# Attention over induced points into a ReLU² MLP: last batch's output chunk by chunk, the closing check moved into the next stage, products earlier, a fourth buffer of x

## The chip, the cores and the metric

The kernel runs on one core of a Trainium2 chip. The metric is device time in microseconds for one execution, as the median of several runs. The engines of the core are named as in the profile: PE (TensorE, matmuls; PEld is its loading of weights), DVE (VectorE), ACT (ScalarE), POOL (GpSimd) and SP (SyncE, which here issues the DMAs). "Clock" is the TensorE clock that the throttle granted, as a share of full speed.

## The reference

Four batches of 12480 rows with 128 features are reduced by attention with 32 inducing vectors, read back by attention, and passed through an MLP with a squared ReLU.

```python
x: (4, 12480, 128) f32    inducing: (32, 128) f32
w_in: (128, 2048)         w_out: (2048, 128)

def mab(q, kv):
    s = scale * (q @ kv.transpose(0, 2, 1))
    s = s - s.max(-1, keepdims=True)
    a = np.exp(s)
    a /= a.sum(-1, keepdims=True) + 1e-09
    return a @ kv
h = mab(I, x)             # (4, 32, 128): 32 rows attend over 12480
y = mab(x, h)             # (4, 12480, 128): each row attends over 32
g = np.maximum(y @ w_in, 0.0) ** 2
out = g @ w_out           # (49920, 128)
```

## The kernel before

Each batch is cut into 26 chunks of 480 rows (`CH`), and its loads into 7 groups `G` of four chunks, the last of two. Two layouts of x are read: `xT` (features on the partitions, tile `xp`) for the scores, and `xn` (rows on the partitions, tile `xn`) for the sum that gives h.

For a batch `b` there is a **first** part (L271): the scores of the 32 inducing vectors (PE at L266, DVE at L281), their maximum, the exponentials on ACT (L304), a transpose on DVE (L313), and `hacc` (PE at L321), which multiplies them with one `xn` tile per group and adds up h in `hq` (L328, L330). `xn` has `XB = 3` buffers: three groups are loaded ahead by `loads`, and group G + 3 is issued behind the matmuls of group G (L325).

Then **prepare** (L374). The MLP is not run column by column. The 32 attention weights of a row are close to equal, so y @ w_in differs little from its mean; hidden columns that can't change sign are treated in closed form. Their squares are a quadratic form in the attention weights, and the kernel builds its matrix `w16` once per batch in four blocks c = 0 to 3: DVE makes products `G` of the 32 columns of h @ w_in with shifted copies of themselves (L544, four instructions a block, and a cast at L546 for the last), and PE multiplies them with w_out (`wq`, L550); DVE or ACT scales the result into `w16`, and DVE takes its largest size `wm` (L552). `G` has two buffers. The few columns that can change sign ("hot") sit in the last 16 rows of block 3. At the end prepare closes a check of the precision (L557 to L574): some nine small DVE instructions on 128x1 values (`wx`, `cm2`), two transposes on PE (L570), and a flag per batch. All flags are read after the last batch; were one zero, a slow way through the whole MLP would be taken instead.

**second** (L351) turns a group's scores into centred f16 attention weights `d16` (ACT at L360 and L364, PE at L367, DVE at L368).

The main loop runs over 13 duos (pairs of chunks) a batch. For each duo there are four steps j in the order 3, 0, 1, 2: `up` multiplies `d16` with a constant matrix of differences into a PSUM tile `hp` of two banks (L593, two buffers); `lift` squares it into `g` (ACT at L602 for j = 0 to 2; for j = 3 DVE makes `tmp` at L606 and POOL squares it at L607). `down` of the duo before adds up the output tile `po`, two banks and one buffer: `lin` for both chunks (L614, 32 rows of the array for each), then for each of four blocks the matmul of both chunks (L618), then one eviction of both chunks, 960 columns, on DVE (L624) for duos below 7 and on ACT (L622) from 7 on, and one store of 480 KB.

Beside this loop `background(b, c)` gives out the work of batch b + 1: each piece is a generator, and `give` advances it to a number of steps that grows with c, the duo plus the quarter. Scores run up to c = 3.5, the rest of the first part up to 6, prepare from 6 on. Text order is only a rank: a planner in the framework turns it into the order on each engine by its own costs, and may put a later instruction first where it expects an engine to be free. Each engine then runs its instructions in order, with waits.

Batch 0 has no loop to hide beside: its first part and prepare run at the start, among the loads and the narrowing of the weights from 64 to 32 bits on DVE (`narrow`, L212 to L224), which uses the pool `start`. That pool is closed before the main loop, and the pool `mlp` takes its place.

## Time and profile before

| | |
|---|---|
| runs | 475.28, 481.98, 489.18 us; median 481.98 |
| profiled execution | 469.63 us, span 467.8 us |
| PE / DVE / ACT / POOL busy | 363.1 / 316.4 / 245.4 / 95.1 us |
| mean granted clock of PE | 0.91 |
| moved by DMA | 81.58 MB |
| start of the main loop's squares | about 100 us |
| last eviction | 457.79 to 458.94 us |

The profile is of one execution. A row of the timeline gives start and duration in us, engine, line, operation, output and inputs, shape and count, and in brackets the engine's idle time before it with what ended it. A row of the waits gives the waiting instruction, the releaser, and the total, the count and the longest in us. Idle time of an engine that isn't on the chain costs nothing. Times of matmuls are pipelined: a matmul of 480 columns shows 0.37 us, but several behind each other follow every 0.2 us.

### The profile page before, as it was taken

Reading aid. Unit: us, or ns where it says so; the run is one execution under the profiler, and the core shown is the slowest. Engines: PE = TensorE matmul, PEld = TensorE weight load, DVE = VectorE, ACT = ScalarE, POOL = GpSimd, SP = SyncE. Lnnn points to the kernel's source line nnn. Section 1 sums busy time; section 2 is a strip of 40 time slices with the busy share of each in tenths; the row PEclk is TensorE's granted clock in tenths of the full one; section 3 lists DMA queues with packets and bytes.
Section 4 is the critical chain, followed back from the end, with each engine's and each line's share of the span. In section 5 each row is a group of like instructions: output and inputs, shape, how many; then the busy total and the mean of one; then the engine's idle time right before and its main releaser. Section 6 shows DMA issues by size and latency. Waiting matters only on the chain.

```text
span 467.8 us, 7805 instructions
## 1 busy us (share of the span) xinstructions
PE 363.1 (78%) x2967; PEld 158.3 (34%) x2967; DVE 316.4 (68%) x836; ACT 245.4 (52%) x338; POOL 95.1 (20%) x62
## 2 busy tenths in 40 slices
PE   3654284598987989889869979799889888888871
PEld 0133141462243424422433346222434264222220
DVE  4779936778675579966755696856755879666420
ACT  1040022634574567765834485565644757676780
POOL 1000000013313113222221121333221222244430
PEclk9986567589999998999998988899999979899997
DMA  8999758000169778122596882222751211232232
GB/s 315 415 401 339 238 197 350 1 1 30 62 234 333 294 277 292 45 84 85 195 312 212 338 285 94 85 85 83 242 183 43 86 42 43 85 127 106 111 125 98
DMA packets 18184, 81.58 MB, mean 174 GB/s; under 512 B 2000, under 2 KB 4048, under 8 KB 18128
## 3 DMA queue, kind: packets, MB, share of 16 engines
q1 hardware_dynamic: 18128, 80.90, 46.9%
q8 instruction: 27, 0.44, 0.4%
q14 instruction: 29, 0.24, 0.2%
HBM read 55.33 MB, written 25.56 MB: 173 GB/s over the span
## 4 chain that ended last, share of the span: by engine, by line
PE 54%; DVE 26%; DMA 9%; ACT 6%; issue 3%; SPq 1%; ACTq 0%; DVEq 0%
PE po L618 15%; PE s L266 12%; PE hp L593 8%; DMA xn<-xn_dram 6%; PE hacc L321 4%; DVE tmp L606 3%; PE hwv L385 3%; DVE G L544 3%; ACT g L602 3%; PE R L495 3%; DMA xp_False<-xT_dram 3%; PE po L614 2%; ACT o L622 2%; PE kv L501 1%; DVE o L624 1%
## 5 line engine op out<-in xcount | busy, mean ns | idle before, releaser
L602 ACT ACTIVATE g<-hp 128x960 f16<-128x960 f32 x156 | 143.1, 969 | 93.7 <-PE hp L593 93.5
L607 POOL TENSOR_TENSOR g<-tmp 128x960 f16<-128x960 f32 x52 | 93.8, 1803 | 357.6 <-DVE tmp L606 242.1
L618 PE MATMUL po<-g,w 128*128 128x480 f16 x416 | 113.0, 380 | 0.0
L606 DVE TENSOR_SCALAR tmp<-hp,off,cut 128x960 f32<-128x960 f32 x52 | 66.1, 1271 | 35.6 <-PE hp L593 35.6
L593 PE MATMUL hp<-d,pairs 32*128 32x480 f16 x312 | 60.9, 377 | 14.9 <-ACT g L602 10.0
L321 PE MATMUL hacc<-xn,en 128*32 128x128 f32 (+1 forms) x840 | 33.8, 303 | 22.4 <-DMA xn<-xn_dram 9.9
L618 PEld LDWEIGHTS <-w 128*128 128x128 f16 x416 | 33.8, 101 | 47.3 <-issue 30.4
L266 PE MATMUL s<-xp_False,indT_sb 128*32 128x480 f32 x208 | 38.5, 701 | 12.2 <-DMA xp_False<-xT_dram 9.8
L172 ACT ACTIVATE s<-s 128x480 f32<-128x480 f32 (+1 forms) x27 | 15.4, 569 | 46.0 <-PE s L266 46.0
L622 ACT ACTIVATE o<-po,bias,osc 128x960 f32<-128x960 f32 x24 | 27.6, 1152 | 20.8 <-PE po L618 20.7
L321 PEld LDWEIGHTS hacc<-xn,en 128*32 128x32 f32 (+1 forms) x840 | 27.0, 120 | 30.7 <-issue 19.9
L593 PEld LDWEIGHTS <-pairs 32*128 32x128 f16 x312 | 14.8, 92 | 66.5 <-issue 65.3
L624 DVE TENSOR_SCALAR o<-po,osc,bias 128x960 f32<-128x960 f32 x28 | 35.4, 1264 | 0.0
L281 DVE TENSOR_SCALAR_CACHE_REDUCE sT<-s 128x480 f32<-128x480 f32 (+1 forms) x28 | 18.3, 654 | 21.4 <-PE s L266 21.3
L304 ACT ACTIVATE sT<-sT,nb 128x480 f32<-128x480 f32 (+1 forms) x28 | 19.1, 682 | 25.3 <-DVE nb L298 25.3
L397 DVE TENSOR_REDUCE bm<-s 128x1 f32<-128x480 f32 (+1 forms) x28 | 18.2, 650 | 19.9 <-ACT s L172 19.6
L266 PE MATMUL s<-xp_False,dhT 128*32 128x480 f32 x208 | 29.2, 648 | 1.2 <-DVE dhT L348 1.2
L544 DVE TENSOR_TENSOR G<-hwp,hw 128x512 f16<-128x512 f16 x64 | 27.9, 458 | 0.7 <-PE wq L550 0.7
L614 PE MATMUL po<-d,lin 32*128 32x480 f16 x104 | 21.0, 367 | 7.8 <-ACT o L622 7.2
L550 PE MATMUL wq<-w_hi,G 128*128 128x128 f16 x256 | 18.4, 230 | 4.0 <-DVE G L546 3.4
L360 ACT ACTIVATE s<-s,nb 128x480 f32<-128x480 f32 (+1 forms) x28 | 17.8, 688 | 5.6 <-DVE k L438 5.6
L330 DVE TENSOR_TENSOR hq<-hacc,hq 128x128 f32<-128x128 f32 x24 | 6.8, 284 | 20.4 <-PE hacc L321 20.2
(227 smaller groups left out, 415.4 us busy)
## 6 DMA issues: line engine op xcount, KB each, us to landing
outT_dram<-o SPq DMA_DIRECT2D x52, 480.0 KB, 2.6
xp_False<-xT_dram SPq DMA_DIRECT2D x24, 960.0 KB, 7.5
xn<-xn_dram SPq DMA_DIRECT2D x24, 960.0 KB, 7.4
wi<-w_in_dram SPq DMA_DIRECT2D x4, 512.0 KB, 13.4
wo<-w_out_dram SPq DMA_DIRECT2D x4, 512.0 KB, 12.0
xp_False<-xT_dram SPq DMA_DIRECT2D x4, 480.0 KB, 6.1
xn<-xn_dram SPq DMA_DIRECT2D x4, 480.0 KB, 9.0
indT_sb<-indT_dram SPq DMA_DIRECT2D x1, 16.0 KB, 1.8
```

The costliest lines, as they stand in the source:

```text
L266: nc.tensor.matmul(ps[32 * q:32 * q + 32, 0:CH], lhsT, xp[:, q, :], start=True, stop=True)
L304: nc.scalar.activation(sT[G][0:r], sT[G][0:r], AF.Exp, bias=nb[0:r], accum_out=st.zs[0:r, G:G + 1])
L321: st.last = nc.tensor.matmul(hacc[c:c + 32, 0:P], en[0:r, k, :], xg[0:r, k, :], start=k < 4, stop=k >= NBLK - 4,)
L544: tt(g[:, :, MI * j:MI * j + n], hwp[:, :, 0:n], hw16f[:, :, s0:s0 + n], op=ALU.mult)
L593: nc.tensor.matmul(hp[:, i, 0:CH], w[r], st.d16[self.G][r], start=True, stop=True)
L602: nc.scalar.activation(self.g[:, j], hp[:, :, 0:CH], AF.Square)
L606: nc.vector.tensor_scalar(tmp, hp[:, :, 0:CH], st.off, cut, op0=ALU.add, op1=ALU.max)
L607: nc.gpsimd.tensor_tensor(self.g[:, j], tmp, tmp, op=ALU.mult)
L614: nc.tensor.matmul(po[:, i, 0:CH], st.lin[r], st.d16[self.G][r], start=True, stop=False)
L618: nc.tensor.matmul(po[:, i, 0:CH], st.w16[:, j], self.g[:, j, i], start=False, stop=n == NC - 1)
L622: nc.scalar.activation(o, po[:, :, 0:CH], AF.Identity, bias=st.bias, scale=st.osc)
L624: nc.vector.tensor_scalar(o, po[:, :, 0:CH], st.osc, st.bias, op0=ALU.mult, op1=ALU.add)
```

## The change

1. `XB` goes from 3 to 4: `loads` fetches four tiles of `xn` ahead, in batch 0 too, and group G + 4 is issued behind the matmuls of group G. For the room `wo_sb` (the narrowed w_out, needed at the start only) moves from the pool `const` to `start`.
2. The products `G` of block 0 are given right behind the scan that ends the preparation of the columns (L475), those of block 1 behind `cat` (L497), and those of block c + 2 behind the matmuls of block c. The buffers of `G` stay two. Prepare now has 25 steps, of which `N_PRE = 26` covers the last.
3. The closing of the check becomes a generator of its own, `closing(b)`, with two steps: the DVE chain is given when batch b's own loop reaches c = 1, the transposes and the flag at c = 2. It was the last part of prepare, ahead of batch b's first duo.
4. For batch 3 `down_singly` takes the place of `down`: lin and the four blocks of chunk 0, its eviction of 480 columns on DVE and its store of 240 KB, then the same for chunk 1, in six steps. The `po` tile and its one buffer stay.

```diff
-XB = 3
+XB = 4
...
-    wo_sb = const.tile([P, NF, P], F32, name="wo_sb")
...
     start = start_pools.enter_context(tc.tile_pool(name="start", bufs=1))
+    wo_sb = start.tile([P, NF, P], F32, name="wo_sb")
...
         nc.vector.tensor_tensor_scan(inc, onec, mix, 0.0, op0=ALU.mult, op1=ALU.add)
         yield
 
+        gs = {}
+
+        def products(c):
+            g = gs[c] = flow.tile([P, NF, P], F16, tag="G", name=f"G_{b}_{c}", bufs=2)
+            for j in range(4):
+                s0 = 4 * c + j + 1
+                n = MI if s0 < 16 else MX
+                tt(g[:, :, MI * j:MI * j + n], hwp[:, :, 0:n], hw16f[:, :, s0:s0 + n], op=ALU.mult)
+            if c == NC - 1:
+                nc.vector.tensor_copy(g[:, :, P - MX:P], hot[:, :, MX:2 * MX])
+
+        products(0)
+        yield
...
         nc.vector.tensor_copy(cat, ps[0:MI + 2, 0:P])
+        products(1)
         yield
...
-        wm = small("wm5", NC)
+        wm = st.wm = small("wm5", NC)
         for c in range(NC):
-            g = flow.tile([P, NF, P], F16, tag="G", name=f"G_{b}_{c}", bufs=2)
-            for j in range(4):
-                s0 = 4 * c + j + 1
-                n = MI if s0 < 16 else MX
-                tt(g[:, :, MI * j:MI * j + n], hwp[:, :, 0:n], hw16f[:, :, s0:s0 + n], op=ALU.mult)
-            if c == NC - 1:
-                nc.vector.tensor_copy(g[:, :, P - MX:P], hot[:, :, MX:2 * MX])
-            yield
             ps = att_psum(f"wq_{b}_{c}")
             for k in range(NF):
-                nc.tensor.matmul(ps[:, 0:P], g[:, k], w_hi[:, k], start=k == 0, stop=k == NF - 1)
+                nc.tensor.matmul(ps[:, 0:P], gs[c][:, k], w_hi[:, k], start=k == 0, stop=k == NF - 1)
             evac(st.w16[:, c], ps[:, 0:P], P, wsc if c < NC - 1 else wsn)
             nc.vector.tensor_reduce(wm[:, c:c + 1], ps[:, 0:P], axis=AX.X, op=ALU.max, apply_absolute_value=True)
             yield
-
+            if c + 2 < NC:
+                products(c + 2)
+                yield
+        st.kept = kv_, rho, pr, cm2
+
+    def closing(b):
+        st = sts[b]
+        tt, ts, stt = nc.vector.tensor_tensor, nc.vector.tensor_scalar, nc.vector.scalar_tensor_tensor
+        kv_, rho, pr, cm2 = st.kept
 
         wx = small("wx")
-        nc.vector.tensor_reduce(wx, wm, axis=AX.X, op=ALU.max)
+        nc.vector.tensor_reduce(wx, st.wm, axis=AX.X, op=ALU.max)
...
+        def down_singly(self):
+            st = self.st
+            po = ps_o.tile([P, 2, 512], F32, tag="po", name=f"po_{self.b}_{self.d}")
+            for i in range(2):
+                r = self.rows(i)
+                nc.tensor.matmul(po[:, i, 0:CH], st.lin[r], st.d16[self.G][r], start=True, stop=False)
+                for n, j in enumerate((3, 0, 1, 2)):
+                    nc.tensor.matmul(po[:, i, 0:CH], st.w16[:, j], self.g[:, j, i], start=False, stop=n == NC - 1)
+                    if n % 2 == 0:
+                        yield
+                o = mlp.tile([P, 2, CH], F32, tag="o", name=f"o_{self.b}_{self.d}_{i}", bufs=3)
+                nc.vector.tensor_scalar(o[:, i], po[:, i, 0:CH], st.osc, st.bias, op0=ALU.mult, op1=ALU.add)
+                nc.sync.dma_start(outT[:, self.b, 2 * self.d + i, :], o[:, i])
+                yield
+
         def down(self):
+            if self.b == NB - 1:
+                yield from self.down_singly()
+                return
...
-    N_LOADS, N_SCORES, N_HEADS, N_PRE, N_SECOND = NG + XB, NG, 2 + 1 + 2 * NG + 2, 7 + 18, 2
+    N_LOADS, N_SCORES, N_HEADS, N_PRE, N_SECOND = NG + XB, NG, 2 + 1 + 2 * NG + 2, 26, 2
...
+    for b in range(NB):
+        gens["c", b] = closing(b)
...
     def background(b, c):
 
+        give(("c", b), 0 if c < 1 else 1 if c < 2 else 2)
```

## The prediction

> **What bounds the kernel now.** I read the page first, then the table by stretches, then the waits, and last the timeline round the places that the change touches.

> ```profile
> span 467.8 us, 7805 instructions
> PE 363.1 (78%) x2967; PEld 158.3 (34%) x2967; DVE 316.4 (68%) x836; ACT 245.4 (52%) x338; POOL 95.1 (20%) x62
> PE 54%; DVE 26%; DMA 9%; ACT 6%; issue 3%; SPq 1%; ACTq 0%; DVEq 0%
> ```

> TensorE (PE) carries over half of the chain and is the busiest engine, at 78%. So the question is where PE stands still. In the next fence the columns are stretch, length, busy time and count of PE, PEld, DVE, ACT and POOL, then the granted clock, the DMA share and GB/s.

> ```profile
> 0.00:40.00 40.00, 19.45 (x175) 7.38 (x175) 28.94 (x104) 6.14 (x15) 1.28 (x10) 0.90 0.97 380
> 110.00:122.00 12.00, 11.70 (x73) 2.75 (x67) 8.88 (x18) 4.93 (x6) 3.39 (x2) 1.00 0.11 42
> 134.00:146.00 12.00, 8.90 (x153) 4.62 (x144) 6.43 (x13) 5.90 (x7) 2.31 (x2) 1.00 0.99 336
> ```

> The start is held by DMA (share 0.97). After it, batch 0's first duos fill PE (11.70 of 12 us), but in the stage that accumulates h of the next batch PE works 8.90 of 12 us while DMA is at 0.99. The waits say for what; the first row is from the waits between 120 and 400 us, the others from the whole span (total us, times, longest).

> ```profile
> PE hacc L321 <- DMA xn<-xn_dram: 9.4, 9, 2.1
> PE cm L570 <- DVE cm L566: 6.7, 4, 2.0
> PE wq L550 <- DVE G L546: 3.4, 4, 1.1
> ```

> Three of the four edits aim at these three rows, 19.5 us together. PE runs its instructions in order, so while it waits on one of them nothing else of it moves.

> **Closing the check a batch later.** In time order, before batch 3:

> ```profile
> 396.91 1.78 POOL L607 TENSOR_TENSOR g<-tmp 128x960 f16<-128x960 f32 x1 [3.37 <-DVE wx L558]
> 397.06 1.65 DVE L560 SCALAR_TENSOR_TENSOR cm<-wx,rho 128x1 f32<-128x1 f32 x1
> 397.86 1.82 ACT L602 ACTIVATE g<-hp 128x960 f16<-128x960 f32 x2
> 399.59 0.27 PE L570 MATMUL cm<-ident,cm 128*1 128x128 f32 x1 [2.00 <-DVE cm L566]
> ```

> A 128x1 operation takes 1.65 us here because it starts 0.15 us after POOL's 1.78 us product and ends with it. The transposes wait for that chain, 2.00 us, and the next duo's matmuls stand behind them. The change gives the chain in duo 1 and the transposes in duo 2 of the batch itself, when the chain is long done, so 6.7 us of waiting can go. What is late next is ACT: its two squares end at 399.68, and only the first frees a PSUM buffer before that (at about 398.8). Hence three quarters, 5.0 us. The chain does not vanish. On DVE it stands ahead of tmp (L606), for which POOL and the PE's next up-matmuls wait. If it meets a POOL product again, it costs 1.65 us; if PE's slack covers it, nothing. Four times half of 1.65 is 3.3 us. Taken: -1.7 us; ends -6.7 (no cost) and +1.6 (5.0 gained, 4 x 1.65 lost).

> **The clock behind the stalls.**

> ```profile
> 200.00:202.00 2.00, 1.94 (x14) 0.52 (x14) 1.23 (x6) 1.04 (x2) 0.00 (x0) 1.00 0.35 138
> 248.00:251.00 3.00, 3.00 (x12) 0.92 (x11) 1.73 (x3) 0.00 (x0) 0.00 (x0) 0.65 0.71 271
> 302.00:304.00 2.00, 2.00 (x12) 0.33 (x5) 0.67 (x2) 0.36 (x1) 0.00 (x0) 0.50 0.00 0
> 400.00:402.00 2.00, 2.00 (x8) 0.35 (x6) 1.01 (x6) 0.53 (x1) 0.00 (x0) 0.58 0.01 2
> 402.00:404.00 2.00, 2.00 (x7) 0.54 (x6) 1.03 (x1) 1.03 (x2) 0.00 (x0) 0.57 0.00 0
> ```

> After the check of two batches (302, 400) and after one wait for xn (248) PE is fully busy at a lowered granted clock; after the check of another batch (200) the clock stays at 1.00. The time lost in these rows is 0.35 x 3 + 0.50 x 2 + 0.42 x 2 + 0.43 x 2 = 3.75 us. One check in three is without a drop, and other stalls remain that can cause one, so I take half, -1.9 us; ends -3.75 and +2 (a new drop such as the pair at 400).

> [...]

> **Four buffers of x for h.**

> ```profile
> 132.34 3.02 SPq L252 DMA_DIRECT2D xn<-xn_dram  x3
> 137.31 1.07 PE L321 MATMUL hacc<-xn,en 128*32 128x128 f32 x30 [1.11 <-DMA xn<-xn_dram]
> 141.01 1.07 PE L321 MATMUL hacc<-xn,en 128*32 128x128 f32 x30 [0.78 <-DMA xn<-xn_dram]
> 144.51 1.07 PE L321 MATMUL hacc<-xn,en 128*32 128x128 f32 x30 [1.21 <-DMA xn<-xn_dram]
> ```

> Three loads go out from 132.34 on, as groups 0 to 2 free their buffers; groups 3, 4 and 5 find them at 137.31, 141.01 and 144.51, each late by 0.78 to 1.21 us. With a fourth buffer group 3 is there beforehand, and the same three loads, at the same instants, serve groups 4, 5 and 6. Group 3 then runs at 137.31 - 1.11 = 136.2; group 4 is wanted 3.70 - 0.78 = 2.9 us later, at 139.1 (there at 137.3); group 5 another 3.50 - 1.21 = 2.3 us on, at 141.4 (there at 141.0). So all the waits can go, though group 5 has only 0.4 us to spare and the DMA share of 0.99 leaves no room: three quarters of 9.4, -7.0 us. Ends: -9.4, and 0 if the saturated DMA merely moves the wait. In batch 0 the fourth tile is loaded ahead of w_out. 0.98 MB at the 380 GB/s of the first row are 2.6 us; narrowing the weights fills DVE for 28.94 of 40 us in that stretch and covers part. Taken: 0, ends -1 and +2.6. Giving up the constant place of wo_sb issues no instruction: 0.

> **Products two blocks ahead.** The order of instructions is the planner's, not that of the text:

> ```profile
> 178.94 0.43 DVE L544 TENSOR_TENSOR G<-hwp,hw 128x512 f16<-128x512 f16 x1
> 179.37 0.18 DVE L475 TENSOR_TENSOR_SCAN inc<-onec,mix 128x16 f32<-128x16 f32 x1
> 189.00 1.07 PE L550 MATMUL wq<-w_hi,G 128*128 128x128 f16 x16
> 191.09 1.27 DVE L606 TENSOR_SCALAR tmp<-hp,off,cut 128x960 f32<-128x960 f32 x1
> 195.45 1.07 PE L550 MATMUL wq<-w_hi,G 128*128 128x128 f16 x16 [0.87 <-DVE G L546]
> ```

> A product already runs ahead of the scan that the text puts first, so for blocks 0 and 1 the edit changes little: 0. Block 3 can differ. Its buffer is free when the second block's matmuls end (190.1), yet DVE takes tmp and more first, and the last matmuls start 0.87 us late. Given ahead of the third block's matmuls, the products can close part of that. Half of 3.4: -1.7 us; ends -3.4 and +1.7 (one block's four products of 0.43 in front of a chain that PE waits for).

> **The last batch chunk by chunk.** A single lin of batch 0, two periods of the last batch, and its end:

> ```profile
> 100.45 0.36 PE L614 MATMUL po<-d,lin 32*128 32x480 f16 x1
> 421.55 1.27 DVE L624 TENSOR_SCALAR o<-po,osc,bias 128x960 f32<-128x960 f32 x1
> 422.87 0.38 PE L614 MATMUL po<-d,lin 32*128 32x480 f16 x2
> 423.18 0.98 PE L618 MATMUL po<-g,w 128*128 128x480 f16 x4
> 424.59 1.28 DVE L606 TENSOR_SCALAR tmp<-hp,off,cut 128x960 f32<-128x960 f32 x1 [1.22 <-PE hp L593]
> 425.79 1.27 DVE L624 TENSOR_SCALAR o<-po,osc,bias 128x960 f32<-128x960 f32 x1
> 442.30 1.15 ACT L622 ACTIVATE o<-po,bias,osc 128x960 f32<-128x960 f32 x1 [0.44 <-PE po L618]
> 446.47 1.15 ACT L622 ACTIVATE o<-po,bias,osc 128x960 f32<-128x960 f32 x1 [0.44 <-PE po L618]
> 455.60 0.38 PE L614 MATMUL po<-d,lin 32*128 32x480 f16 x2 [1.24 <-ACT o L622]
> 457.79 1.15 ACT L622 ACTIVATE o<-po,bias,osc 128x960 f32<-128x960 f32 x1 [2.24 <-PE po L618]
> ```

> The period is a loop through the one po buffer: eviction, lin at 422.87 right behind its end, eight matmuls, eviction again. It is 4.24 us with DVE and 4.17 us with ACT. For a PSUM tile of 480 columns DVE takes 0.65:

> ```profile
> L281 DVE TENSOR_SCALAR_CACHE_REDUCE sT<-s 128x480 f32<-128x480 f32 (+1 forms) x28 | 18.3, 654 | 21.4 <-PE s L266 21.3
> ```

> With one buffer I let the next lin wait until both chunks of the tile before are evicted; the first chunk's eviction lies beside the second chunk's matmuls, and only the second's, 0.65, is left in the loop. Against that, lin no longer runs as a pair: one alone takes 0.36 where the pair takes 0.38 together, so the second adds up to the 0.31 between 422.87 and 423.18, with no cover. That is -0.62 + 0.31 = -0.31 us for the duos evicted by DVE, -0.50 + 0.31 = -0.19 for those of ACT, about -0.25 for each of 12 periods: -3.0 us. If lin waits for its own chunk alone, the eviction leaves the loop: 12 x (0.31 - 1.2) = -10.7; the other end is the slower rival's +11. ACT's lost evictions cost nothing; DVE then has 1.28 + 2 x 0.65 = 2.6 us of work in a period of 4. At the end the last eviction shrinks by 0.50, the 1.24 us wait at 455.60 by as much, and a lin is added: -0.7 us, ends -1.3 and +0.3. SP issues 26 stores of half the size in place of 13, with no load left beside them: 0.

> [...]

> **Sum.** -1.7 - 1.9 - 7.0 - 1.7 - 3.0 - 0.7 = -16.0 us. The profiled execution took 469.63 us, 1.83 us more than its span: 453.6. The median of the runs shown is 481.98, 1.026 times the profiled execution, so the forecast on that scale is 466 us, 3.4% less.

> **Rivals.** *Everything that waits goes*: check 6.7, xn 9.4, products 3.4, clock 3.75, last batch and end 3.7: -27 us, 443 on the profile's scale, 454 on the median's. For it: PE is in order and nearly full elsewhere (11.70 of 12). Against it: other waits stand close behind each, as the ACT squares do. Chance 0.10.

> *The gaps fill up again*: the planner pulls the closing chain forward to where it stood (it had moved products ahead on its own), and at a DMA share of 0.99 the fourth buffer only shifts the wait. What remains are the last batch and a third of xn's: -3.0 - 0.7 - 3.1 = -7 us; 474. For it: the share of 0.99, and text order that doesn't bind. Against it: the computed spare at groups 4 and 5, and that the planner ranks what is given late behind what is given early. Chance 0.27.

> *Slower*: in the last batch DVE now holds tmp and both evictions. If the second chunk's eviction is regularly queued behind tmp, the loop gets about 1.28 us longer than forecast, 4.0 + 1.28 = 5.2 in place of 4.24: 12 x 0.96 = +11 us. For it: already now the eviction at 425.79 starts only as the tmp of 424.59 ends. Against it: in the text the second chunk's last matmul precedes the next tmp. It makes the kernel slower from the point at which the other edits give less than 11 us; with nothing of theirs, 481 us on the profile's scale, 493 on the median's. Chance 0.11.

> That leaves 0.52 for the forecast. I count 2% (9.6 us) as what a measurement of this kernel, whose three runs span 475 to 489, can tell from no change.

> **How the numbers follow.** Of the forecast's 0.52 some 0.46 lie beyond 2%, the rest within, since each of its large terms could halve. With the first rival faster has 0.56; the second rival and the 0.06 make 0.33 for within 2%; slower 0.11. The forecast's own ends, terms halved or met in full, are 474 and 454. The range runs from 453, just under the first rival, to 483, where the second rival has lost its last gain; above it lies most of the slower rival, below it half of the first.

> **What would show it.** Right: the row of hacc waiting for xn shrinks from 9.4 us between 120 and 400 us to under 3; cm waiting for cm falls from 6.7 to under 1, and the clock stays at 1.00 round the batch changes; the period of the last batch is 3.8 to 4.1 us with evictions of 0.65. Wrong: transposes of the check still at the batch change; hacc waits of the old length; DVE's half evictions starting at the end of a tmp, with a period over 4.3; or a first lin (at 100.45 now) that comes more than 2.6 us later. The prediction fails above all if PE's removed waits come back under other names, which the waits view would list.

## The result: 4.7% slower, with the last batch at half the clock

The changed kernel takes 494.53 us (median of 4, 493.23 to 500.08), the kernel before in the same comparison 478.63 (471.63 to 489.18): a ratio of 1.047, with an interval of 1.032 to 1.062. Forecast were 466 us. The ratios here and below compare only the executions of each kernel within 1.5% of its own fastest, so they are not the quotients of the medians, and a kernel with few executions is set against the fastest of many of before. The profiled execution took 493.23 us; that of before, 469.63 us, was faster than all four timed ones, so the profiles lie further apart (23.6 us by their spans) than the medians (15.9 us).

From the page of the kernel after:

```profile
span 491.4 us, 7847 instructions
PE 402.7 (82%) x2967; PEld 160.4 (33%) x2967; DVE 322.5 (66%) x854; ACT 240.5 (49%) x333; POOL 94.8 (19%) x62
PEclk9566595789998699999895999998958975555555
PE 62%; DVE 22%; DMA 7%; issue 3%; ACT 3%; SPq 1%; DVEq 0%; ACTq 0%
L635 DVE TENSOR_SCALAR o<-po,osc,bias 128x480 f32<-128x480 f32 x26 | 20.2, 777 | 51.9 <-PE po L631 51.9
```

PE has the same 2967 matmuls and is busy 39.6 us longer. The PEclk row (40 slices, the clock in tenths) shows where: its last seven slices are all 5. Stretches of the kernel after, with the columns of the table by stretches in the prediction:

```profile
134.00:146.00 12.00, 9.52 (x97) 4.03 (x97) 7.03 (x14) 4.40 (x5) 2.20 (x2) 1.00 0.94 310
394.00:398.00 4.00, 3.63 (x18) 0.97 (x17) 3.03 (x5) 2.56 (x3) 1.23 (x1) 1.00 0.48 179
395.92:399.33 3.41, 2.31 (x12) 0.55 (x12) 3.14 (x4) 1.58 (x3) 0.92 (x1) 1.00 0.26 89
400.00:402.00 2.00, 2.00 (x6) 0.41 (x5) 0.00 (x0) 1.17 (x2) 0.20 (x1) 0.50 0.30 116
430.00:468.00 38.00, 36.21 (x102) 7.30 (x102) 15.96 (x18) 14.25 (x16) 9.14 (x6) 0.50 0.20 72
```

The last batch starts at clock 1.00. At 399.33, in its first duos, the clock falls, and it never comes back, though PE is shown busy for 36.21 of 38 us. In the window before it (395.92 to 399.33) PE waits 0.36 us for an eviction, and then 0.83 us for ACT, until 399.42. Of the first three edits two took their waits away and the fourth buffer shortened its own: the first lin of the last batch comes at 394.0 us instead of 405.5, and the transposes of the check no longer wait:

```profile
387.83 0.16 DVE L581 TENSOR_TENSOR cm<-cm,wx 128x1 f32<-128x1 f32 x1
389.55 0.38 PE L585 MATMUL cm<-ident,cm 128*1 128x128 f32 x2
```

(The planner pulled the chain forward to 386.55, ahead of the loop after all, but it now ends 1.6 us before its transposes.) But from first lin to the end of the last eviction the last batch takes 87.6 us in place of 53.5: -11.4 + 34.1 = +22.7, against +23.6 between the spans. Two chunks of that batch, PE and evictions:

```profile
419.38 0.78 DVE L635 TENSOR_SCALAR o<-po,osc,bias 128x480 f32<-128x480 f32 x1 [1.18 <-PE po L631]
420.21 0.55 PE L629 MATMUL po<-d,lin 32*128 32x480 f16 x1
423.14 0.78 DVE L635 TENSOR_SCALAR o<-po,osc,bias 128x480 f32<-128x480 f32 x1 [2.43 <-PE po L631]
423.97 0.56 PE L629 MATMUL po<-d,lin 32*128 32x480 f16 x1
424.46 1.78 PE L631 MATMUL po<-g,w 128*128 128x480 f16 x4
426.28 0.78 DVE L635 TENSOR_SCALAR o<-po,osc,bias 128x480 f32<-128x480 f32 x1 [1.18 <-PE po L631]
427.11 0.55 PE L629 MATMUL po<-d,lin 32*128 32x480 f16 x1 [0.36 <-DVE o L635]
```

The period of a duo is 427.11 - 420.21 = 6.90 us, where the old order had 4.24. And each lin starts 0.05 us behind the end of an eviction (419.38 + 0.78 = 420.16), that of the chunk just before it. The last experiment comes back to this.

### The profile page after: what moved, and what is told of

It reads as the page before. It is cut to its first block, busy times and chain, and to the rows that moved or that the text cites. A ratio compares the mean times of both kernels' runs of the same rounds, so it can differ in the third digit from the quotient of the medians.

```text
span 491.4 us, 7847 instructions
## 1 busy us (share of the span) xinstructions
PE 402.7 (82%) x2967; PEld 160.4 (33%) x2967; DVE 322.5 (66%) x854; ACT 240.5 (49%) x333; POOL 94.8 (19%) x62
## 4 chain that ended last, share of the span: by engine, by line
PE 62%; DVE 22%; DMA 7%; issue 3%; ACT 3%; SPq 1%; DVEq 0%; ACTq 0%
PE s L266 12%; PE po L651 12%; PE hp L608 10%; PE po L631 9%; DMA xn<-xn_dram 5%; PE hacc L321 3%; PE hwv L385 3%; PE po L629 3%; DVE tmp L621 3%; DMA xp_False<-xT_dram 2%; PE R L509 2%; DVE G L485 2%; DVE o L635 2%; PE wq L557 2%; ACT g L617 2%
## 5 line engine op out<-in xcount | busy, mean ns | idle before, releaser
L617 ACT ACTIVATE g<-hp 128x960 f16<-128x960 f32 x156 | 144.8, 968 | 108.7 <-PE hp L608 75.3
L622 POOL TENSOR_TENSOR g<-tmp 128x960 f16<-128x960 f32 x52 | 93.5, 1798 | 374.2 <-DVE tmp L621 93.0
L651 PE MATMUL po<-g,w 128*128 128x480 f16 x312 | 89.2, 403 | 0.0
L608 PE MATMUL hp<-d,pairs 32*128 32x480 f16 x312 | 68.4, 425 | 9.9 <-ACT g L617 7.5
L621 DVE TENSOR_SCALAR tmp<-hp,off,cut 128x960 f32<-128x960 f32 x52 | 66.2, 1274 | 12.5 <-PE hp L608 12.0
L635 DVE TENSOR_SCALAR o<-po,osc,bias 128x480 f32<-128x480 f32 x26 | 20.2, 777 | 51.9 <-PE po L631 51.9
L321 PE MATMUL hacc<-xn,en 128*32 128x128 f32 (+1 forms) x840 | 34.3, 307 | 19.2 <-DMA xn<-xn_dram 14.1
L266 PE MATMUL s<-xp_False,indT_sb 128*32 128x480 f32 x208 | 37.4, 665 | 12.9 <-DMA xp_False<-xT_dram 8.7
L631 PE MATMUL po<-g,w 128*128 128x480 f16 x104 | 47.1, 581 | 0.0
L651 PEld LDWEIGHTS <-w 128*128 128x128 f16 x312 | 25.7, 103 | 40.6 <-issue 27.9
L321 PEld LDWEIGHTS hacc<-xn,en 128*32 128x32 f32 (+1 forms) x840 | 27.7, 122 | 26.7 <-issue 20.8
L266 PE MATMUL s<-xp_False,dhT 128*32 128x480 f32 x208 | 31.2, 695 | 3.2 <-DVE dhT L348 3.0
L397 DVE TENSOR_REDUCE bm<-s 128x1 f32<-128x480 f32 (+1 forms) x28 | 18.2, 650 | 22.7 <-ACT s L172 22.5
L281 DVE TENSOR_SCALAR_CACHE_REDUCE sT<-s 128x480 f32<-128x480 f32 (+1 forms) x28 | 18.3, 654 | 20.7 <-PE s L266 20.5
L655 ACT ACTIVATE o<-po,bias,osc 128x960 f32<-128x960 f32 x18 | 20.7, 1150 | 19.0 <-PE po L651 19.0
L657 DVE TENSOR_SCALAR o<-po,osc,bias 128x960 f32<-128x960 f32 x21 | 26.5, 1262 | 1.2 <-PE po L651 1.2
L608 PE MATMUL hp<-d,pair 32*128 32x480 f16 x104 | 25.0, 431 | 1.0 <-ACT g L617 1.0
L631 PEld LDWEIGHTS <-w 128*128 128x128 f16 x104 | 10.5, 123 | 41.1 <-issue 40.9
```

What stands on the lines that cost most here:

```text
L266: nc.tensor.matmul(ps[32 * q:32 * q + 32, 0:CH], lhsT, xp[:, q, :], start=True, stop=True)
L321: st.last = nc.tensor.matmul(hacc[c:c + 32, 0:P], en[0:r, k, :], xg[0:r, k, :], start=k < 4, stop=k >= NBLK - 4,)
L608: nc.tensor.matmul(hp[:, i, 0:CH], w[r], st.d16[self.G][r], start=True, stop=True)
L617: nc.scalar.activation(self.g[:, j], hp[:, :, 0:CH], AF.Square)
L621: nc.vector.tensor_scalar(tmp, hp[:, :, 0:CH], st.off, cut, op0=ALU.add, op1=ALU.max)
L622: nc.gpsimd.tensor_tensor(self.g[:, j], tmp, tmp, op=ALU.mult)
```

## The experiments

Two questions stood at the start: is it the chunk order of the last batch, and what in it; and what does the clock go by. "After" and "before" are the two kernels of the result. Before's median lay between 475.3 and 480.3 us in all comparisons.

### The order of the last batch

**Old `down` in the last batch (e1)**, all else as after:

```diff
         def down(self):
-            if self.b == NB - 1:
-                yield from self.down_singly()
-                return
```

> The changed kernel with the old order of the last batch: lin of both chunks, then block by block for both, one eviction of 960 columns on DVE or ACT; the other three edits stay. Theory A, that the chunk order alone puts the last batch on half clock: granted clock about 1.00 from the first output matmul of batch 3 to the end, period 4.2 us, mean clock 0.9 or more, and the time is some 11 us below the kernel before (the changed kernel reached its first lin of batch 3 at 394.0 where the kernel before had 405.4), ratio about 0.976. Rival B, that the denser first three batches bring the clock down later: the last batch stays at 0.50 here too, period 5.5 us or more, ratio 1.0 or above.

**Before with the chunk order alone (e2)**: `down_singly` and its call put into before.

> The kernel before with the last batch's chunk order alone. Theory A: clock 0.50 through the last batch, period 6.9 us, the last batch (first lin to last eviction) 87 us where it was 53.5, ratio about 1.07. Rival B: clock 1.00, period about 4, ratio about 0.99.

Measured: e1 461.14 us, ratio 0.982 (0.964 to 1.000); e2 506.16, ratio 1.081 (1.061 to 1.101). The PEclk rows of e1 and, in the second fence, of e2:

```profile
PEclk9566587679998969999989889998889569999997
```

```profile
PEclk9955595799999999999899889899899855555555
```

So the loss comes with the chunk order alone; nothing of the other three edits is needed for it. How the clock fell differs, though. Two windows of e2, whose first chunk-wise lin comes at 402.62:

```profile
394.98:398.39 3.41, 1.88 (x11) 0.54 (x11) 2.88 (x13) 2.06 (x3) 0.63 (x1) 1.00 0.36 144
398.39:401.81 3.42, 3.42 (x12) 0.79 (x11) 1.32 (x2) 2.25 (x4) 1.04 (x1) 0.50 0.00 0
```

Here the clock falls at 398.39, before the chunk order begins, behind a wait of 2.01 us for the check. Before has the same wait and the same fall, at 400.31, but is back at 1.00 at 403.72. So e2 shows that the chunk order keeps the clock from returning. That it can also lose the clock is shown by after, which falls in its first chunk-wise duos where e1 does not, and by e4 and e8 below.

**Lins as a pair (e3)**: both lins of a duo first, the rest chunk by chunk.

```diff
             for i in range(2):
                 r = self.rows(i)
                 nc.tensor.matmul(po[:, i, 0:CH], st.lin[r], st.d16[self.G][r], start=True, stop=False)
+            for i in range(2):
                 for n, j in enumerate((3, 0, 1, 2)):
```

> The changed kernel with the two lin matmuls of a duo again side by side, ahead of chunk 0's four blocks; the rest of the chunk order stays, so a tile is still evicted in two halves. If the single lin (32 rows of the array alone, one more change of mode) keeps the clock down: clock 1.00 in the last batch and a period of 4.0, time about 455 to 465. If the wait for the eviction at each duo does it: clock 0.50, period 6.5 or more, time over 485.

**One `po` tile for the whole last batch (e4)**:

```diff
-            po = ps_o.tile([P, 2, 512], F32, tag="po", name=f"po_{self.b}_{self.d}")
+            if self.d == 0:
+                st.po = ps_o.tile([P, 2, 512], F32, tag="po", name=f"po_{self.b}")
+            po = st.po
```

> The changed kernel with one po tile for the whole last batch, so that a chunk's lin need wait only for the eviction of the same chunk of the duo before. If the wait for the eviction keeps the clock down: the idle time of lin behind DVE (5.8 us in 12 waits) goes, clock 1.00, period 3.7 to 4.0, time about 455 to 460. If the single lin does it: the waits go, but the clock stays at 0.50 and the period at 6.3 or more, time over 480.

e3: 472.23 us, 1.004 (0.994 to 1.013), clock 1.00 through the last batch, period 4.69 us. e4: 493.6, 1.054 (1.032 to 1.075). e4 starts its last batch at the full clock and shows the fall; stretches and, below, two rows of its timeline:

```profile
404.00:408.00 4.00, 3.17 (x16) 0.94 (x15) 2.13 (x3) 2.32 (x3) 1.78 (x1) 1.00 0.36 131
412.00:416.00 4.00, 3.81 (x18) 0.94 (x15) 2.39 (x3) 2.02 (x3) 1.02 (x1) 0.88 0.23 86
420.00:424.00 4.00, 4.00 (x12) 0.85 (x11) 2.09 (x3) 2.63 (x3) 1.79 (x1) 0.50 0.31 117
```

```profile
408.29 0.78 DVE L637 TENSOR_SCALAR o<-po,osc,bias 128x480 f32<-128x480 f32 x1 [2.12 <-PE po L633]
409.12 0.36 PE L631 MATMUL po<-d,lin 32*128 32x480 f16 x1 [0.21 <-DVE o L637]
```

At the full clock e4's period is 4.70 us (lins at 414.92 and 419.62), 5.46 in its first duos: slower than the old order's 4.24 before the clock falls. It falls at 410, returns, falls at 420 and stays. But the edit had not done its work: the lin still starts at the end of the eviction of the chunk before, so e4 says nothing on that wait. From e3 I concluded too early that the lone lin was to blame.

**Old order of matmuls, but two evictions and two stores (e5)**, and **chunk order in the very last duo alone (e6)**:

> After, with the old order of matmuls in the last batch (both lins, then the products of both chunks side by side), but still two evictions of 480 columns on DVE and two stores. If the lone lin of the chunk order is what halves the clock: last batch at clock 1.00, period about 4.2 us, and the time that of the run with the old down, 461 us, changed by the splitting alone: 0.777 x 2 - 1.262 = +0.3 us of DVE a duo at most (+4), -0.6 at the end: 460 to 465. If the two evictions and stores were what opens the gaps: clock 0.50 and about 494.

> After, with the chunk order for the very last duo alone. The clock has no time to fall in one duo: last batch at 1.00, the run with the old down (461 us, 0.982 of before) less what the split of the last eviction and store takes from the end (0.65 us was my estimate, 1.15 - 0.777 and a shorter store by the rows): 460, 0.98 of before. Rival: one lone lin is enough to halve the clock for the last 4 us: 463.

e5: 467.59 us, 0.975 (0.966 to 0.984), clock 1.00, period 4.42: the halved evictions do no harm to the clock. e6: 462.48, 0.975 (0.970 to 0.981), no better than e1's 461.14. Its last duo takes 4.80 us from lin to the last eviction's end (446.30 to 451.10) where before's took 3.34, because its second lin waits 0.93 us for the first chunk's eviction.

**Chunk order late (e8) or early (e9)** in the last batch: `if self.b == NB - 1 and self.d >= 6`, and `self.d < 6`.

> After, with the old down for the first six duos of the last batch and the chunk order from the seventh on. If the chunk order itself loses the clock: 1.00 until the seventh duo, 0.50 some 5 to 20 us behind it and to the end; 7 duos x up to (6.9 - 4.2) = +19 on 461: about 476 to 480. Rival, that only the pause at the batch's start (2 us of PE at 398) throws the clock and the loop merely cannot win it back: 1.00 to the end, 7 x (5.4 - 4.2) = +8: 469.

> After, with the chunk order for the first six duos of the last batch and the old down from the seventh on. If the chunk order keeps itself at the half clock and the old order does not: 0.50 over the first six duos, back to 1.00 within one or two duos of the change, 461 + 6 x 2.7 = 477. Rival, that a clock once halved late in the run stays so whatever the order: 0.50 to the end and 488 to 494.

e8 (469.54 us, 0.976, 0.969 to 0.982), then e9 (478.24, 1.007, 0.999 to 1.014):

```profile
430.00:433.41 3.41, 3.23 (x17) 0.87 (x17) 2.16 (x3) 1.45 (x3) 0.50 (x2) 1.00 0.39 142
433.41:436.82 3.41, 2.66 (x14) 0.62 (x11) 1.63 (x3) 2.62 (x3) 1.69 (x1) 0.99 0.21 79
436.82:440.24 3.42, 3.06 (x9) 0.64 (x8) 1.69 (x2) 1.40 (x2) 1.38 (x1) 0.50 0.20 72
```

```profile
441.20:444.62 3.42, 3.09 (x11) 0.76 (x10) 1.28 (x1) 1.92 (x3) 1.76 (x1) 0.50 0.01 2
444.62:448.03 3.41, 3.41 (x10) 0.61 (x9) 0.18 (x1) 1.92 (x3) 0.03 (x1) 0.50 0.36 144
448.03:451.44 3.41, 2.86 (x16) 0.82 (x14) 1.10 (x1) 2.78 (x4) 1.79 (x1) 1.00 0.24 96
```

In e8 the clock falls at 436.8, in the middle of the loop, 16 us after the first chunk-wise lin (420.4), with no PE wait above 0.6 us in between. (The pause of 2 us in the expectation's rival is, in the timeline of after, the wait of 0.83 us that ends at 399.42.) The loop's period there is 4.70. Its time is nonetheless the rival's 469: the fall came so late that it cost little. In e9 the old order begins at the half clock at 431.7 and is back at 1.00 at 448, after 16 us, not one or two duos. So the chunk order keeps the half clock, and the old order leaves it.

### What the clock goes by

**More work: a thrown-away matmul ahead of each lin (e7)**

```diff
+                nc.tensor.matmul(po[:, i, 0:CH], st.w16[:, 3], self.g[:, 3, i], start=True, stop=True)
                 nc.tensor.matmul(po[:, i, 0:CH], st.lin[r], st.d16[self.G][r], start=True, stop=False)
```

> After, with one more matmul of 128 rows x 480 columns ahead of each lin in the last batch; its sum is thrown away, since the lin that follows starts the sum anew. It adds 2 full-row matmuls a duo and removes no switch between 32 and 128 rows (it adds some). Theory 1, the clock goes by the work of full rows per time (old order 8 matmuls of 128 rows in 4.2 us and the paired lin 8 in 4.69 keep the full clock, the chunk order 8 in about 5.4 at full clock loses it): 10 in about 5.6 keep it, last batch 13 x 5.6 = 73 us instead of 88, so about 479 us: more work, less time. Theory 2, it goes by the number of switches, or by how long 32-row matmuls stand alone: clock 0.50 as before, 2 x 0.4 us more a duo: 494 + 10 = 504.

**All-zero matmuls, eight a duo (e10)**

```diff
+                    nc.tensor.matmul(po[:, i, 0:CH], zeros16, self.g[:, j, i], start=False, stop=False)
                     nc.tensor.matmul(po[:, i, 0:CH], st.w16[:, j], self.g[:, j, i], start=False, stop=n == NC - 1)
```

> After, chunk order, with one matmul of an all-zero weight (128 rows x 480 columns, adds zero to the sum) ahead of each of the eight products of a duo, inside the same stretches of 128-row matmuls: no more switches between 32 and 128 rows, lone lins as before, twice the 128-row work. Theory 1, the clock goes by the 128-row work per time (old 8 x 0.2 us in 4.2 = 0.38, paired lin 1.6 in 4.69 = 0.34, both at 1.00; chunk order 1.6 in 5.4 = 0.30, falls; at half clock 1.6 in 6.9 = 0.23, stays; the thrown-away matmul 2.0 in 7.9 = 0.25, stays): here 3.2 in about 6.5 = 0.49, clock 1.00, last batch 13 x 6.5 = 85 us, about 491. Theory 2, the lone 32-row matmul itself halves it: 0.50 and a period of 6.9 + 8 x 0.4 = 10.1: 536.

**The old order slowed by ACT (e11)**: in the last batch ACT's squares for j = 0 and 1 are done twice.

> After, with the old down in the last batch, and there two of ACT's three squares of each duo done twice (the same values again). No lone lin, no added switch, no added matmul: only the period grows, from 4.2 to some 5.5 us, PE waiting for ACT. Theory 1 (128-row work per time): 1.6 in 5.5 = 0.29, the clock falls in the last batch as in the chunk order, though nothing of the order is there. Theory 2 (the lone lin, or the order): 1.00 throughout, 461 + 13 x 1.3 = 478.

**Each pair of hp twice in the last batch (e16)**: `for i in range(4 if self.b == NB - 1 else 2)` in `up`, with `i % 2`.

> After, chunk order, with each pair of 32-row matmuls of the first layer (hp) issued twice in the last batch, the same values again: 8 more 32-row matmuls a duo behind their likes, no more switches, 128-row work unchanged. Theory 1 (128-row work per time): 1.6 in 5.4 or more, below 0.30: clock 0.50, period 6.9 + 4 pairs x 0.4 = 8.5, last batch 110 us: about 515. Rival, that any matmul which fills PE's gaps keeps the clock, as the zero matmuls did: 1.00 and about 485.

**All-zero matmuls, two a duo (e17)**: as e10, at j = 0 alone.

> After, chunk order, with two all-zero 128-row matmuls a duo in place of eight, inside the stretches of 128 rows. Theory 1: 10 x 0.2 us in about 5.6 = 0.36, above the 0.34 at which the paired lin kept 1.00: clock 1.00, last batch 13 x 5.6 = 73 us, about 480. If it falls: the border lies above 0.36 on this path or the share is not the measure; 0.50, period 7.7, about 505.

Rows of e7, e10, e11, e16 and e17, in this order:

```profile
396.00:400.00 4.00, 3.17 (x13) 0.84 (x12) 2.14 (x3) 1.83 (x2) 1.79 (x1) 1.00 0.34 128
400.00:404.00 4.00, 3.98 (x14) 1.06 (x14) 1.96 (x2) 1.67 (x2) 0.00 (x0) 0.60 0.18 62
```

```profile
420.00:430.00 10.00, 8.52 (x42) 2.63 (x41) 4.39 (x7) 5.05 (x6) 3.04 (x2) 1.00 0.20 75
```

```profile
436.00:440.00 4.00, 1.33 (x6) 0.29 (x6) 1.28 (x1) 4.00 (x6) 0.83 (x1) 0.83 0.00 0
440.00:444.00 4.00, 3.96 (x16) 1.27 (x16) 0.00 (x0) 3.51 (x5) 1.78 (x1) 0.50 0.31 123
```

```profile
416.00:420.00 4.00, 3.79 (x21) 1.12 (x21) 2.68 (x4) 2.19 (x3) 1.19 (x1) 1.00 0.25 92
```

```profile
420.00:428.00 8.00, 7.06 (x34) 2.13 (x33) 4.26 (x6) 5.42 (x7) 2.84 (x2) 1.00 0.25 92
```

e7 503.92 to 508.66 us, median 505.98 (ratio 1.065, 1.057 to 1.072): half clock. e10, one execution: 487.33, clock 1.00, period 6.32 us in place of 6.90: 104 added matmuls, and 7 us less than after. e16, one execution: 474.49, clock 1.00, period 5.52 us: 104 added matmuls of 32 rows, and 20 us less than after. (The kernels ran in different comparisons; the periods are the surer sign.) e17, two executions, 481.70: clock 1.00 until the last duos. e11, one execution, 482.3: it falls for some us after waits of 0.90 us, returns, and after the pause at 436 to 440 stays at half for about 24 us, with no lone lin in it.

As I had put it, theory 1 missed in e7, which added 128-row matmuls and had the half clock, and falls with e16, which added none and kept the clock. A lone lin as the cause falls with e10, e16 and e17, which kept all of them, and with e11. Averages over a period don't settle it either: e3 keeps the clock at 4.69 us, e8 loses it at 4.70 with the same matmuls.

So single windows have to be compared. In the traces the clock changes only at multiples of 3.41 us, as in the two fences above (in before it stands at 0.50 from 400.31 to 403.72). I cut the main loop of all twenty profiles into those windows, took the 657 that hold f16 matmuls only, and counted in each the matmuls that start there, in units of one with 128 rows and 480 columns (32 rows count a quarter, fewer columns in proportion). Against that stands the clock of the next window:

| work in a window | from 1.00: stays / falls | from 0.50: returns / stays |
|---|---|---|
| under 5.9 | 2 / 21 | 3 / 134 |
| 5.9 to 6.4 | 16 / 17 | 5 / 19 |
| 6.4 to 6.9 | 15 / 0 | 1 / 6 |
| 6.9 and more | 388 / 2 | 27 / 1 |

Counted without regard to rows, the same windows don't separate: from the half clock it returned after 16 of 79 windows with under 9 units, and after none of 23 with 11 or more. In the rows of e8 above the window from 433.41 holds 4 matmuls of 128 rows and 8 of 32, work 6.0, and the clock falls behind it; in e9 the window from 444.62 holds 6 and 4, work 7.0, and it returns.

Counted in windows that begin and end 0.225 us earlier (681 of them, between the first and the last matmul into `po`), the borders for falling and returning become one, near 6.5:

| work, window 0.225 us earlier | from 1.00: stays / falls | from 0.50: returns / stays |
|---|---|---|
| under 6.0 | 0 / 39 | 0 / 143 |
| 6.0 to 6.5 | 2 / 15 | 0 / 18 |
| 6.5 to 7.0 | 18 / 3 | 5 / 5 |
| 7.0 and more | 406 / 0 | 27 / 0 |

The first fall of e4 shows the difference: the window before it holds 7.0 units by the first count and 6.0 by the second. The 0.225 us, the weights and the border were all chosen on these same windows, and no run was made to test them. A border at 6.5 leaves 10 windows on the wrong side; with a weight of 0 or a half for 32 rows even the best borders leave 27 or 28, with 0.15 or 0.35 they leave 13 or 12. So in these windows a count in which 32 rows weigh less fits better, the quarter only roughly; what the throttle itself goes by is not shown. By the first count, in the last batch:

| last batch | work per window at 1.00: mean, least | at 0.50: mean, most |
|---|---|---|
| e1 | 8.7, 7.5 | - |
| e3 | 7.8, 6.25 | - |
| e4 | 7.6, 5.75 | 5.2, 6.25 |
| e7 | 6.2 (one window) | 5.3, 6.25 |
| after | 5.25 (the window that it falls behind) | 5.2, 5.75 |
| e9 | 7.8, 7.5 | 5.6, 7.0 |
| e10 | 10.0, 8.75 | - |
| e16 | 7.8, 6.25 | - |
| e17 | 8.4, 5.75 | 5.2, 5.25 |

The same count, applied to the slow loop: a duo holds 8 + 10 / 4 = 10.5 units. At the full clock the chunk order's 4.70 us give 10.5 x 3.41 / 4.70 = 7.6 a window on average, but single windows reach down to 6. At the half clock the period is 6.90 us a duo, 5.2 a window, and no window of after got beyond 5.75 (6.25 by the second count); in the first table the clock returned after 3 of 137 windows under 5.9. The old order at the half clock (e9, 6.0 us a duo) has 6.0 on average, and got its one window of 7.0, behind which the clock returned, after 16 us. In e7 the two added matmuls make it 12.5 units in 7.95 us, 5.4 a window: more work, but slower in the same measure. e3 and e16 kept the clock with 6.25 in their thinnest windows. Without its zeros e10 would have 10.5 x 3.41 / 6.32 = 5.7 a window on average, and the clock fell behind 21 of 23 windows under 5.9; with them it has 10.0 and stayed at 1.00, which speaks for counting the zeros. PE's busy share says little of this: 2.66 of 3.41 us in the window of e8 that lost the clock, 3.41 of 3.41 in many windows of after that stay at half.

### Why the chunk order is thin

**A PSUM tile of its own for the second chunk (e18)**, one of the attention's two, nearly idle in the last batch:

```diff
+                acc = po[:, 0, 0:CH] if i == 0 else att_psum(f"po_{self.b}_{self.d}_1")[:, 0:CH]
-                nc.tensor.matmul(po[:, i, 0:CH], st.lin[r], st.d16[self.G][r], start=True, stop=False)
+                nc.tensor.matmul(acc, st.lin[r], st.d16[self.G][r], start=True, stop=False)
```

(and `acc` in the four matmuls and the eviction).

> After, chunk order, with the second chunk's sum in a PSUM tile of its own (of the two that the attention uses, nearly idle in the last batch). In the run with one shared tile each lin still started at the very end of the eviction of the chunk before it (409.07 and 409.12). If that wait, two evictions of 0.78 us in the loop of a duo, is what thins the loop: lins no longer wait for DVE, a period of 4.5 or less (18 matmuls in 4.5 = 4.0 per us, where 3.84 kept the clock), clock 1.00, 458 to 463. If the lone lins and switches thin it: period near 5.4, clock 0.50, about 494.

458.75 us (451.22 to 459.94, 4 executions) beside 479.90 for before (466.47 to 487.59, 7 executions): 4.4% less by the medians, with no overlap; no interval came with it. It is the fastest median of the study, and it is the change as it was made, with lone lins and chunk order. A stretch of its last batch, then its timeline:

```profile
420.00:430.00 10.00, 9.74 (x48) 2.88 (x45) 7.88 (x10) 6.03 (x8) 3.72 (x3) 1.00 0.35 124
```

```profile
419.74 0.78 DVE L636 TENSOR_SCALAR o<-po,osc,bias 128x480 f32<-128x480 f32 x1 [0.88 <-PE po L632]
419.85 0.36 PE L630 MATMUL po<-d,lin 32*128 32x480 f16 x1
421.47 0.37 PE L630 MATMUL po<-d,lin 32*128 32x480 f16 x1
421.62 0.77 DVE L636 TENSOR_SCALAR o<-po,osc,bias 128x480 f32<-128x480 f32 x1
423.76 0.36 PE L630 MATMUL po<-d,lin 32*128 32x480 f16 x1
```

The waits of lin for evictions in after, then all that is listed of PE's waits in e18 between 394 and 448 us (total, times, longest):

```profile
PE po L629 <- DVE o L635: 5.8, 12, 0.9
```

```profile
PE hp L608 <- ACT g L617: 1.0, 4, 0.3
```

A lin now starts while the chunk before it is being evicted (419.85 within 419.74 to 420.52). The periods are 3.91 (419.85 to 423.76) and, the next one, 4.07 us, 3.99 on average, and the work in a window is 9.4 on average and never under 9.0, at the full clock. So the wait of each lin for the other chunk's eviction thinned the loop, and the thin loop could not hold the clock. The edit takes out two such waits at once, that of the second chunk's lin for the first chunk's eviction and that of the next duo's first lin for the second's; they were not tried apart. What holds the period at 3.99 us now is PE itself, busy for 9.74 of 10 us. From the second duo's first lin to the last eviction e18 takes 47.0 us (400.96 to 447.94), e1 with the old order 48.8 (402.55 to 451.32): freed of the waits, the chunk order gains some 2 us.

### The other three edits

**Before with the fourth buffer alone (e12)**; **e6 with three buffers (e13)**, so closing and products without the buffer; **e13 with the products back in the loop (e14)**, so closing alone; **e13 with the check in its old place (e15)**, so products alone.

> Before, with four buffers of x for h and the output weights' tile in the pool of the start, and nothing else of the change. My prediction gave this part -7.0 us (the longest waits of PE for xn gone, 9.4 us to under 3 between 120 and 400 us). The profile of after shows 7.0 us of that wait left, so -2 to -3 is what I expect now; the rival, that with two buffers free the loads come earlier and the waits go to the loads of xT, gives 0.

> The version with the chunk order in the last duo alone (462.48, 0.975 of before), with three buffers of x for h and the output weights' tile back in its own place: closing and products without the fourth buffer. If the buffer is worth nothing, as it was alone: 460 to 463, 0.97 to 0.98. If it is worth the -7.0 of my sum once the stalls behind it are gone: 469, 0.99.

> As the one before, and the products G back in the loop in front of their own matmuls: of the three edits only the last check a batch later (closing) is left. My sum: closing -1.7 and the clock behind the stalls -1.9, tail -0.7: 0.99. Rival, that the 11 us come from the boundary between the batches, where the closing and what is behind it are drained before the next batch's first step: most of the gain is here, 0.98.

> Three buffers, chunk order in the last duo alone, products G two blocks ahead, the last check in its old place with the old pace of the planner (25 units). My sum: -1.7 and -0.7: 0.995. Rival, that the products are what shortens the boundary: 0.98.

| edits | median | before's median | quotient | ratio to before, as above |
|---|---|---|---|---|
| buffer (e12) | 478.29 | 475.58 | 1.006 | 1.018 (1.010 to 1.026) |
| closing (e14) | 477.39 | 477.78 | 0.999 | 1.003 (0.994 to 1.011) |
| products (e15) | 478.63 | 477.78 | 1.002 | 1.025 (1.012 to 1.038) |
| closing and products (e13) | 473.13 | 477.78 | 0.990 | 1.005 (0.999 to 1.011) |
| all three (e6) | 462.48 | 475.58 | 0.972 | 0.975 (0.970 to 0.981) |

e13 to e15 have the chunk order in the last duo, as e6. None gains alone; together they gain 2 to 3%. That the buffer or the products alone make it slower is not shown: the medians differ by 0.6 and 0.2%. PE's wait for xn between 120 and 390 us in before, e12, e13 and e6 (total, times, longest):

```profile
PE hacc L321 <- DMA xn<-xn_dram: 9.4, 9, 2.1
```

```profile
PE hacc L321 <- DMA xn<-xn_dram: 6.3, 6, 1.8
```

```profile
PE hacc L321 <- DMA xn<-xn_dram: 6.8, 6, 1.9
```

```profile
PE hacc L321 <- DMA xn<-xn_dram: 4.8, 5, 1.6
```

The wait shrinks with either and most with all, but in e12 it saves nothing in the end. Where e12's 3 us went is not settled: the granted clock between 120 and 390 us was 0.96 in before's profile and 0.91 in e12's, but 0.92 in e6's too, and before's own executions range more widely than that.

## Why the prediction was wrong

The range ended at 483 us; 494.5 lies above it. By the steps of the prediction:

**Closing (-1.7).** The waits on cm went, as said; the planner did pull the chain forward, as the second rival had it, but without a wait behind it. Alone the edit brought nothing that can be measured (e14).

**The clock behind the stalls (-1.9, worst +2).** The term looked for falls behind stalls only. The row with 0.50 at 302 stood behind a wait of 2.00 us (until 300.44) just as the row at 400 did; and 0.58 and 0.65 are only stretches that mix 1.00 and 0.50, the two values that the traces hold. The falls in e4 and e8 came with no PE wait above 0.83 us; what went with them was the work in a window. In e4 the clock falls at 410, returns, falls again at 420 and then stays down; in after it did not return for 82 us (399.33 to 481.3) in which PE is shown busy 93% of the time, with 5.2 units a window.

**xn (-7.0).** The wait fell from 9.4 to 7.0 us in after, not under 3. Alone the buffer was worth nothing (e12), with the others some 10 us (e13 against e6, from two comparisons). The sum treated as separate what only pays together; why it does is not shown. The three edits' total of -12.3 us (closing, clock, xn, products) was nearly right, -11.4 at the first lin of the last batch and a ratio of 0.975 in e6, but with none of its parts borne out alone that is partly luck.

**Products (-1.7).** The waits of wq for G went, but alone the edit gains nothing that can be measured (e15).

**Last batch (-3.0).** This is the step that failed: "only the second's, 0.65, is left in the loop". I let lin wait for the tile before, and forgot that the second chunk's lin waits for the first chunk's eviction in the same tile. Both evictions are in the loop, each of 0.777 us, not 0.65: 1.55 us in place of the old order's 1.27, with PE idle or thin around them. The full-clock period became 4.70 us (e4, e8) instead of 3.99, and, once a thin window had cost the clock, 6.90. That the loop itself could lose the clock was in no term and in no rival. With the waits gone (e18) the period is 3.99, which equals the forecast 4.24 - 0.25, but by luck: the forecast had kept the wait for the second chunk's eviction. For a lin that waits for its own chunk alone, as in e18, the prediction had -10.7 us, a period of 4.24 - 0.89 = 3.35; it left out that PE is full at 3.99 (busy for 9.74 of 10 us in e18). The slower rival had the right side and the wrong mechanism: no eviction was queued behind tmp, and its +11 us were a third of the 34.1.

For a lin that no longer runs as a pair the step added 0.31 us, read from 422.87 to 423.18 in before. In e18 between 400 and 445 us a matmul of 480 columns starts 0.21 us (median) behind another of 128 rows, and 0.30 to 0.31 us when 32 rows follow 128 or 128 follow 32. So a change took about 0.1 us there, and a lone lin between 128-row matmuls 0.3 + 0.3 - 0.2 = 0.4 us by this sum.

**Tail (-0.7).** With one tile the last duo got longer, 4.80 us against 3.34 (e6); with tiles of their own it takes 3.33 (444.61 to 447.94 in e18), so the shorter last eviction gained nothing. The span ends 9.96 us behind the last eviction there, against 8.86 before; over all profiles this end lies between 8.7 (e16, halved stores) and 10.1 us (e11, whole ones), so no gain or loss of the halved stores shows in it.

## What to carry to other kernels

When a step is cut in halves that share a buffer, draw the loop again with every release and every wait: here the halves waited for each other. A loop on PE must be priced at the clock that it holds: here a loop that was 11% slower (4.70 against 4.24 us) ended 63% slower (6.90), with PE shown busier than before. In this kernel, where the clock stayed at 0.50 with PE shown "busy", the number to look at was the matmuls in a window of 3.41 us, weighted by their rows, against a stage that held 1.00 (5.2 in after, 8.7 in e1); the next question was what thinned them.
